# Pacing the sums of weight quarters and splitting the transposes of k and q in a fused retention and MLP kernel

## The chip, the cores and the metric

The kernel runs on one core of one Trainium2 chip. The metric is the device time in microseconds (us), lower is better; a time given for a kernel is the median of its runs. The engines are TensorE (PE, its weight loads PEld), VectorE (DVE), ScalarE (ACT), GpSimd (POOL) and SyncE (SP, which issues the transfers).

## The reference

A retention block (8 batches, 8 heads, 576 positions, head dimension 64) feeds an MLP with a parametric relu, all in float32:

```python
def _attn_ref(q, k, v):                       # q, k, v: (8, 8, 576, 64)
    scores = scale * np.matmul(q, k.transpose(0, 1, 3, 2))
    gamma = 1.0 - 2.0 ** (-5.0 - np.arange(H, dtype=np.float32))
    rel = pos[:, None] - pos[None, :]
    Dmat = np.where(rel >= 0, gamma[:, None, None] ** rel[None, :, :], 0.0)
    return np.matmul(scores * Dmat[None], v)

x = np.ascontiguousarray(attn_out.transpose(0, 2, 1, 3)).reshape(B * S, H * D)   # (4608, 512)
h = x @ w_in                                  # (4608, 2048)
g = np.maximum(h, 0.0) + alpha * np.minimum(h, 0.0)
out = g @ w_out                               # (4608, 512)
```

## The kernel before

The tokens go through the MLP in 18 blocks of 256. Blocks 0 and 1 are multiplied plainly (`plain_unit`, `plain_out`), while the weights are still being loaded and rounded piece by piece (`piece_in` on ScalarE, `piece_out` on VectorE and GpSimd). Every later block uses seven products in the place of eight (`mlp_unit`, the scheme of Strassen and Winograd), and for that the weights need sums and differences of their quarters, which GpSimd makes in place. A block is eight units; a unit is 28 matmuls into `ph` (each float32 product counts as two in the profile), the work on `g`, and 14 matmuls into `po`. The retention goes by pairs of heads, numbered over all batches: pairs 0 to 3 belong to the first batch, 4 to 7 to the second, and so on. Pairs 4 to 7 are computed in the gaps of a loop of 12 plain units, in a fixed order of instructions; pairs 8 to 31 run in a later loop between units of the seven-product kind.

In the excerpts a comment such as `# L304` marks the line under which the profile counts an instruction.

The loads and the sums of the weight quarters. Each quarter of the weights (two units) brings 12 sums, four on `w_in` and eight on `w_out`:

```python
    NEARLY = 2 * NPAIR            # NPAIR = 4
    # ... (cut; load_sq loads in squares of 32 x 32, rows of 32 floats; load_nat in rows of 64)
    def load_pair(n):
        b, c = pairs[n]
        kn, vn, qx = [nat.tile([P, NM, 2, D], FP32, tag=f"nat_{x}", name=f"{x}n_{n}")
                      for x in "kvq"]
        if n < NEARLY:
            kx = kn
            load_nat(kn, k, b, c)
            load_nat(qx, q, b, c)
        else:
            kx = nat.tile([P, NB, 32], FP32, tag="sq_k", name=f"kx_{n}")
            qx = qx.rearrange("p m h d -> p (m h d)")[:, 0:S].rearrange(
                "p (n r) -> p n r", r=32)
            load_sq(kx, k, b, c)
            load_sq(qx, q, b, c)
            load_nat(kn, k, b, c)
        load_nat(vn, v, b, c)
        return kn, kx, qx, vn
    # ... (cut)
    waiting = []
    def combine(n):
        for _ in range(min(n, len(waiting))):
            w, (o, x, y, op) = waiting.pop(0)
            nc.gpsimd.tensor_tensor(out=w[:, o], in0=w[:, x], in1=w[:, y], op=op)  # L304
    S_WORK = ((1, 0, 1, ALU.subtract), (5, 3, 1, ALU.subtract), (4, 5, 0, ALU.add),
              (6, 2, 5, ALU.subtract))
    T_WORK = ((1, 3, 1, ALU.subtract), (5, 1, 0, ALU.add), (4, 3, 5, ALU.subtract),
              (6, 2, 5, ALU.subtract))
    # ... (cut; at the end of plain_out(kb, i, g), after its matmuls into po (L372):)
        if kb == PLAIN[-1] and i % UST == UST - 1:
            waiting.extend((w_in[i // UST], x) for x in S_WORK)
            waiting.extend((w_out[j], x) for j in range(i + 1 - UST, i + 1) for x in T_WORK)
            if i == NU - 1:
                combine(len(waiting))
```

A unit of the seven-product kind (its weights are `w_in[i // 2]` and `w_out[i]`), and the differences of a block's input, which GpSimd makes:

```python
    def combine_x(kb):            # four GpSimd subtractions 128x256 (L425)
        # ... (cut)
    def mlp_unit(kb, i):
        if kb not in xt:
            combine_x(kb)
        x, t = xb[kb], xt[kb]
        ph = [ps_h.tile([P, 4, P], FP32, tag=f"psh{m}", name=f"ph{m}_{kb}_{i}")
              for m in range(2)]
        for n, (m, o, l, r) in enumerate((
                (0, 2, 0, x[:, 0:2, 0:P]), (0, 0, 2, x[:, 2:4, 0:P]), (0, 1, 5, t[:, 1]),
                (1, 0, 4, t[:, 0]), (1, 1, 1, x[:, 0:2, P:TB]),
                (1, 2, 6, x[:, 2:4, P:TB]), (1, 3, 3, t[:, 2]))):
            for cc in range(2):
                nc.tensor.matmul(ph[m][:, o], w_in[i // UST][:, l, i % UST, cc], r[:, cc],  # L439
                                 start=(n in (0, 3) and cc == 0), stop=(n in (2, 6) and cc == 1),
                                 skip_group_check=True)
        g = mlp.tile([P, 8, P], FP32, tag="g", name=f"g_{kb}_{i}")
        nc.scalar.copy(g[:, 7], ph[0][:, 2])  # L445
        for o, x0, x1 in ((g[:, 0:5:4], ph[0][:, 0:2], g[:, 7:8].to_broadcast([P, 2, P])),
                          (g[:, 5:7], ph[1][:, 0:2], g[:, 4:5].to_broadcast([P, 2, P])),
                          (g[:, 3], ph[1][:, 0], g[:, 6]),
                          (g[:, 1:3], ph[1][:, 2:4], g[:, 5:7])):
            nc.vector.tensor_tensor(out=o, in0=x0, in1=x1, op=ALU.add)  # L450
        for m in range(2):
            fc = m * NU + i
            nc.vector.tensor_scalar(g[:, 4 + 2 * m:6 + 2 * m], g[:, 2 * m:2 * m + 2], 0.0,  # L453
                                    alpha[:, fc:fc + 1], ALU.min, ALU.mult)
        nc.vector.scalar_tensor_tensor(  # L455
            out=g[:, 0:4].rearrange("p x t -> p (x t)"),
            in0=g[:, 0:4].rearrange("p x t -> p (x t)"), scalar=0.0,
            in1=g[:, 4:8].rearrange("p x t -> p (x t)"), op0=ALU.max, op1=ALU.add)
        for o, x0, x1, op in ((4, 1, 3, ALU.add), (6, 0, 1, ALU.subtract),
                              (5, 4, 0, ALU.subtract), (7, 2, 5, ALU.subtract)):
            nc.vector.tensor_tensor(out=g[:, o, :], in0=g[:, x0, :], in1=g[:, x1, :], op=op)  # L461
        pend.append((kb, i, g))
        if len(pend) > 1:
            mlp_out()
```

The retention of a pair in its steps, scale, transposes (t), scores (s), states (u) and values (v). The PSUM tiles of all of them share two buffers (`psa`):

```python
    def scale(t, x, c):            # t times its decay factors, two GpSimd multiplications (L510)
        # ... (cut)
    def ps_tile(shape, name):
        return ps_a.tile(shape, FP32, tag="psa", name=name)
    def scale_pair(n):
        c = pairs[n][1]
        scale(loaded[n][2], 0, c)
        scale(loaded[n][3], 1, c)
    def transposes(n):
        c = pairs[n][1]
        kn, kx, qx, vn = loaded[n]
        kT = attn.tile([P, S], FP32, tag="kT", name=f"kT_{n}")
        qT = attn.tile([P, S], FP32, tag="qT", bufs=2, name=f"qT_{n}")
        if n < NEARLY:
            for src, dst in ((kn, kT), (qx, qT)):
                for x, (m0, m1) in enumerate(((0, 3), (3, NM))):
                    w = min(m1 * P, S) - m0 * P
                    pt = ps_tile([P, 3 * P], f"pt{m0}_{n}")
                    for m in range(m0, m1):
                        rows = min(P, S - m * P)
                        nc.tensor.transpose(  # L535
                            pt[:, (m - m0) * P:(m - m0) * P + rows],
                            src[0:rows, m].rearrange("p h d -> p (h d)"),
                            ident[0:rows, 0:rows])
                    nc.scalar.copy(dst[:, m0 * P:m0 * P + w], pt[:, 0:w])  # L539
        else:
            qh = qx.rearrange("p (j x) r -> p j x r", x=2)
            nc.gpsimd.tensor_tensor(out=qh, in0=qh,  # L542
                                    in1=tabx[:, None, c, :, None].to_broadcast([P, NJ, 2, 32]),
                                    op=ALU.mult)
            scale(vn, 1, c)
            for src, dst in ((kx, kT), (qx, qT)):
                nc.vector.transpose(dst, src.rearrange("p n r -> p (n r)"))  # L547
        return kT, qT
    # ... (cut)
    def scores(n, kT, qT):        # two PSUM tiles "psa", 40 matmuls (L565), then
        # ... (cut)               # two DVE operations on them (L569)
    def states(n, kn, vn):
        c = pairs[n][1]
        ps = [ps_tile([P, NM - 1, D], f"pu{p2}_{n}") for p2 in range(2)]
        for m in range(NM - 1):
            for p2 in range(2):
                for h2 in range(2):
                    nc.tensor.matmul(ps[p2][half(h2), m], kn[half(p2), m, h2],  # L580
                                     vn[half(p2), m, h2], start=(m == 0), stop=(m == NM - 2),
                                     skip_group_check=True)
        su = attn.tile([P, NJ - 1, D], FP32, tag="su", bufs=2, name=f"su_{n}")
        g1, g2 = gch[:, 0, c:c + 1], gch[:, 1, c:c + 1]
        nc.scalar.copy(su[:, 0::2], ps[0])  # L585
        nc.vector.scalar_tensor_tensor(out=su[:, 1::2], in0=su[:, 0::2], scalar=g1, in1=ps[1],  # L586
                                       op0=ALU.mult, op1=ALU.add)
        for j in range(3, NJ - 1, 2):
            nc.vector.scalar_tensor_tensor(out=su[:, j], in0=su[:, j - 2], scalar=g2,  # L589
                                           in1=su[:, j], op0=ALU.mult, op1=ALU.add)
        nc.vector.scalar_tensor_tensor(out=su[:, 2::2], in0=su[:, 1:NJ - 3:2], scalar=g1,  # L591
                                       in1=ps[0][:, 1:], op0=ALU.mult, op1=ALU.add)
        return su
    # ... (cut; values: two PSUM tiles "psa", matmuls L604 and L611, then ScalarE copies into xb)
```

The loop of 12 plain units, and the one after it:

```python
    # ... (cut; step("v", n) calls values and then loads pair n + 2)
    steps = [(x, n) for n in range(NPAIR, NEARLY) for x in "tsuv"]
    scale_pair(NPAIR)
    scaled = [NPAIR + 1]
    def gap():
        for x, n in steps[0:3]:
            if x == "t" and n == scaled[0] and n in loaded:
                scaled[0] += 1
                step("scale", n)
        if steps:
            step(*steps.pop(0))
            if not steps:
                combine_x(len(PLAIN))
    units = [(kb, i) for i in range(UST, NU) for kb in PLAIN]
    for n, (kb, i) in enumerate(units):
        plain_unit(kb, i)
        plain_relu()
        if n >= 1:
            gap()
        piece_in(1)
        piece_out(1)
        mlp_out()
        combine(1)
        piece_in(1)
        if n >= 4 or n == 2:
            gap()
        piece_out(1)
        combine(1)
    assert not steps
    ordered.close()
    tc.no_sync_barrier()
    enqueue(0)
    enqueue(1)
    turned = {}
    for n, (b, c) in enumerate(pairs):
        if n < NEARLY:
            continue
        if n + 1 < len(pairs):
            loaded[n + 1] = load_pair(n + 1)
        kn, _, _, vn = loaded[n]
        share = -(-len(queue) // (NPAIR - c))
        cuts = [(share + i) // 3 for i in range(3)][::-1]
        kT, qT = turned.pop(n) if n in turned else transposes(n)
        at = scores(n, kT, qT)
        pop_units(cuts[0])
        su = states(n, kn, vn)
        pop_units(cuts[1])
        if n + 1 < len(pairs):
            turned[n + 1] = transposes(n + 1)
        values(n, vn, qT, at, su)
        del loaded[n]
        pop_units(cuts[2])
```

Of the kernel before, what the change touches and what calls it, by code (L numbers as in the profile page):

```python
# [10 lines left out]
FP32 = mybir.dt.float32  # L11
# [3 lines left out]
ALU = mybir.AluOpType  # L15
# [3 lines left out]
def kernel(  # L19
# [10 lines left out]
    nc = tc.nc  # L30
    B, H, S, D = q.shape
    NTOK, DM = out.shape
    DFF = moe_w_in.shape[1]
    P = 128

    NPAIR = H // 2
    C = 64
    NJ = S // C
    NM = (NJ + 1) // 2
# [3 lines left out]
    NU = NFC // 2  # L43
# [4 lines left out]
    UST = NU // NST  # L48
# [19 lines left out]

    NEARLY = 2 * NPAIR

# [87 lines left out]
    ident = const.tile([P, P], FP32, name="ident")  # L162
# [135 lines left out]

    waiting = []

    def combine(n):
        for _ in range(min(n, len(waiting))):
            w, (o, x, y, op) = waiting.pop(0)
            nc.gpsimd.tensor_tensor(out=w[:, o], in0=w[:, x], in1=w[:, y], op=op)  # L304

    S_WORK = ((1, 0, 1, ALU.subtract), (5, 3, 1, ALU.subtract), (4, 5, 0, ALU.add),
              (6, 2, 5, ALU.subtract))
# [58 lines left out]
    def plain_out(kb, i, g):  # L366
        if i == 0:
            acc[kb] = [ps_o.tile([P, DM], FP32, tag=f"pso{2 * kb + m}", name=f"po{m}_{kb}")
                       for m in range(2)]
        for m in range(2):  # L370
            for x in range(2):
                nc.tensor.matmul(acc[kb][m], g[:, 2 * x + m],  # L372
                                 w_out[i][:, 2 * x:2 * x + 2].rearrange("p x f -> p (x f)"),
                                 start=(i == 0 and x == 0), stop=(i == NU - 1 and x == 1))
        if i == NU - 1:
            po = acc.pop(kb)
            osb = ring.tile([P, 2, DM], FP32, tag=f"o{kb}", name=f"osb_{kb}")
            for m in range(2):
                t0 = kb * TB + m * P
                nc.scalar.copy(osb[:, m], po[m])  # L380
                nc.sync.dma_start(out[t0:t0 + P, :], osb[:, m])
        if kb == PLAIN[-1] and i % UST == UST - 1:
            waiting.extend((w_in[i // UST], x) for x in S_WORK)
            waiting.extend((w_out[j], x) for j in range(i + 1 - UST, i + 1) for x in T_WORK)
            if i == NU - 1:
                combine(len(waiting))

    def plain_unit(kb, i):

# [37 lines left out]
# [31 lines that stand above are left out]
            in1=g[:, 4:8].rearrange("p x t -> p (x t)"), op0=ALU.max, op1=ALU.add)  # L458
        for o, x0, x1, op in ((4, 1, 3, ALU.add), (6, 0, 1, ALU.subtract),
                              (5, 4, 0, ALU.subtract), (7, 2, 5, ALU.subtract)):  # L460
            nc.vector.tensor_tensor(out=g[:, o, :], in0=g[:, x0, :], in1=g[:, x1, :], op=op)  # L461
        pend.append((kb, i, g))
        if len(pend) > 1:
            mlp_out()
# [50 lines left out]
    def ps_tile(shape, name):  # L515
        return ps_a.tile(shape, FP32, tag="psa", name=name)
# [6 lines left out]
    def transposes(n):  # L523
        c = pairs[n][1]
        kn, kx, qx, vn = loaded[n]
        kT = attn.tile([P, S], FP32, tag="kT", name=f"kT_{n}")
        qT = attn.tile([P, S], FP32, tag="qT", bufs=2, name=f"qT_{n}")
        if n < NEARLY:
            for src, dst in ((kn, kT), (qx, qT)):
                for x, (m0, m1) in enumerate(((0, 3), (3, NM))):  # L530
                    w = min(m1 * P, S) - m0 * P
                    pt = ps_tile([P, 3 * P], f"pt{m0}_{n}")
                    for m in range(m0, m1):
                        rows = min(P, S - m * P)
                        nc.tensor.transpose(  # L535
                            pt[:, (m - m0) * P:(m - m0) * P + rows],
                            src[0:rows, m].rearrange("p h d -> p (h d)"),
                            ident[0:rows, 0:rows])
                    nc.scalar.copy(dst[:, m0 * P:m0 * P + w], pt[:, 0:w])  # L539
        else:  # L540
            qh = qx.rearrange("p (j x) r -> p j x r", x=2)
            nc.gpsimd.tensor_tensor(out=qh, in0=qh,  # L542
                                    in1=tabx[:, None, c, :, None].to_broadcast([P, NJ, 2, 32]),
                                    op=ALU.mult)
            scale(vn, 1, c)
            for src, dst in ((kx, kT), (qx, qT)):
                nc.vector.transpose(dst, src.rearrange("p n r -> p (n r)"))  # L547
        return kT, qT

    def half(x):  # L550
        return slice(x * C, (x + 1) * C)
# [252 lines left out]
    plain_unit(0, 1)  # L804
    piece_out(1)
    plain_relu()
    part_values(1)
    part_carry(1)
    piece_in(1)
    last_transposes()  # L810
    mlp_out()
    piece_out(1)
# [20 lines left out]
    def step(what, n):  # L833
        kn, _, _, vn = loaded[n]
        if what == "scale":
            scale_pair(n)
        elif what == "t":
            kq[n] = transposes(n)
        elif what == "s":
            ats[n] = scores(n, *kq[n])  # L840
        elif what == "u":
            sus[n] = states(n, kn, vn)
        elif what == "v":
            values(n, vn, kq[n][1], ats[n], sus[n])
            del loaded[n]
            if n + 2 <= NEARLY:
                loaded[n + 2] = load_pair(n + 2)

    steps = [(x, n) for n in range(NPAIR, NEARLY) for x in "tsuv"]
    scale_pair(NPAIR)  # L850
    scaled = [NPAIR + 1]

    def gap():

        for x, n in steps[0:3]:
            if x == "t" and n == scaled[0] and n in loaded:
                scaled[0] += 1
                step("scale", n)
        if steps:
# [3 lines that stand above are left out]
# [3 lines left out]
# [7 lines that stand above are left out]
        mlp_out()  # L873
        combine(1)
        piece_in(1)
        if n >= 4 or n == 2:
            gap()
        piece_out(1)
        combine(1)
    assert not steps  # L880
    ordered.close()
    tc.no_sync_barrier()
# [2 lines left out]

    turned = {}
    for n, (b, c) in enumerate(pairs):
        if n < NEARLY:
            continue
        if n + 1 < len(pairs):  # L890
            loaded[n + 1] = load_pair(n + 1)
# [13 lines that stand above are left out]
        if c == NPAIR - 1:  # L905
            enqueue(b)
# [31 lines left out]
```

## Time and profile before

| what | value |
|---|---|
| time, median of 3 runs | 1065.72 us (1065.14 to 1067.84) |
| span of the profiled execution | 1063.5 us |
| PE busy | 1026.0 us |
| DVE busy | 765.0 us |
| POOL busy | 215.2 us |
| ACT busy | 171.1 us |
| moved by DMA | 63.36 MB |

A row of the table of groups reads: line, engine, operation, the tile written and those read, shape, count, then busy time, mean time of one, and the idle time of the engine just before. In a timeline, a row begins with its start and its length in us, and ends, in brackets, with the idle time ahead of it and what ended it; several instructions alike are merged. In the chain of waits each step is what released the step after it.

### The profile page before, as it was taken

The numbers are of one execution on the slowest core, as the hardware profiler recorded it, in microseconds if no ns is written. First come the engines' busy times: TensorE is split into PE (matmuls) and PEld (weight loads), VectorE is DVE, ScalarE is ACT, GpSimd is POOL, SyncE is SP. The second block draws the span as 40 slices with busy tenths as digits, with TensorE's granted clock in tenths as the row PEclk, the third lists the DMA queues.
The fourth block names the chain that finished last, engine by engine and source line by source line (L and its number), as shares of the span: only waits on it lengthen the run. The fifth ranks groups of instructions, "written<-read, shape, count | busy, mean of one in ns | idle before, by whom it ended". The sixth has DMA issues, their size and how long they took to land.

```text
span 1063.5 us, 27061 instructions
## 1 busy us (share of the span) xinstructions
PE 1026.0 (96%) x11329; PEld 903.3 (85%) x11329; DVE 765.0 (72%) x1951; ACT 171.1 (16%) x533; POOL 215.2 (20%) x253
## 2 busy tenths in 40 slices
PE   6899997699999999999999999999999999999998
PEld 5666565699999999999999999999999999999997
DVE  7757656877787778676777777777768676767575
ACT  4445541111011111001101111111111111000000
POOL 4455659301120102111103011201120000100000
PEclk9999999799999999999999999999999999999999
DMA  9855504113222222111212222131222100000000
GB/s 244 242 143 155 147 21 107 33 38 77 47 64 46 66 45 56 34 43 35 55 24 55 47 46 66 38 73 36 66 47 55 24 22 1 21 1 22 1 21 20
DMA packets 216073, 63.36 MB, mean 60 GB/s; under 512 B 201088, under 2 KB 209296, under 8 KB 215952
## 3 DMA queue, kind: packets, MB, share of 16 engines
q1 hardware_dynamic: 213840, 61.11, 24.7%
q8 instruction: 89, 1.46, 0.6%
q10 hardware_dynamic: 2112, 0.53, 0.3%
q14 instruction: 32, 0.26, 0.1%
HBM read 52.17 MB, written 9.44 MB: 58 GB/s over the span
## 4 chain that ended last, share of the span: by engine, by line
PE 92%; DVE 4%; issue 1%; POOL 1%; DMA 1%; ACT 0%; SPq 0%; DVEq 0%; POOLq 0%; ACTq 0%
PE ph L439 39%; PE po L357 36%; PE po L372 4%; PE ph L395 4%; PE pv L611 2%; PE ps L565 2%; PE pv L604 2%; DVE g L453 2%; PE pu L580 2%; DMA w_out<-in_k_dram 1%; DVE su L589 1%; DMA kn<-in_k_dram 0%; POOL w_in L294 0%; POOL w_out L294 0%; PE pt L535 0%
## 5 line engine op out<-in xcount | busy, mean ns | idle before, releaser
L357 PE MATMUL po<-w_out,g 128*128 128x256 f32 x1792 | 409.6, 380 | 14.8 <-DVE g L455 14.8
L357 PEld LDWEIGHTS po<-w_out,g 128*128 128x128 f32 x1792 | 332.0, 191 | 55.1 <-DVE g L455 15.0
L450 DVE TENSOR_TENSOR g<-ph,g 128x256 f32<-128x256 f32 (+1 forms) x512 | 187.4, 387 | 179.9 <-PE ph L439 94.9
L439 PE MATMUL ph<-xb,w_in 128*128 128x128 f32 x2048 | 277.6, 278 | 0.0
L439 PEld LDWEIGHTS ph<-xb,w_in 128*128 128x128 f32 x2048 | 253.2, 192 | 9.2 <-issue 1.0
L439 PE MATMUL ph<-xt,w_in 128*128 128x128 f32 x1536 | 213.6, 275 | 0.0
L439 PEld LDWEIGHTS ph<-xt,w_in 128*128 128x128 f32 x1536 | 192.2, 192 | 0.1
L461 DVE TENSOR_TENSOR g<-g 128x128 f32<-128x128 f32 x512 | 142.4, 319 | 7.8
L453 DVE TENSOR_SCALAR g<-g,alpha 128x256 f32<-128x256 f32 x256 | 109.8, 471 | 4.5
L510 POOL TENSOR_TENSOR vn<-vn,th 128x512 f32<-128x512 f32 (+1 forms) x56 | 39.8, 731 | 355.1 <-DMA vn<-in_v_dram 279.1
L445 ACT COPY g<-ph 128x128 f32<-128x128 f32 x128 | 34.1, 266 | 461.7 <-PE ph L439 448.6
L455 DVE SCALAR_TENSOR_TENSOR g<-g 128x512 f32<-128x512 f32 x128 | 91.7, 717 | 3.8
L395 PE MATMUL ph<-xb,w_in 128*128 128x256 f32 x256 | 60.3, 390 | 1.9 <-ACT xb L725 1.4
L372 PE MATMUL po<-w_out,g 128*128 128x512 f32 x128 | 58.8, 602 | 0.8 <-DVE g L411 0.8
L395 PEld LDWEIGHTS ph<-xb,w_in 128*128 128x128 f32 x256 | 48.9, 194 | 11.4 <-issue 4.3
L425 POOL TENSOR_TENSOR xt<-xb,xt 128x256 f32<-128x256 f32 x32 | 25.2, 789 | 162.8 <-ACT xb L500 162.2
L498 ACT COPY xb<-pv 64x64 f32<-64x64 f32 (+1 forms) x144 | 34.0, 236 | 145.7 <-PE pv L611 143.9
L372 PEld LDWEIGHTS po<-w_out,g 128*128 128x128 f32 x128 | 23.3, 190 | 25.0 <-issue 21.8
L411 DVE SCALAR_TENSOR_TENSOR g<-g,nalpha,ph 128x256 f32<-128x256 f32 x32 | 13.9, 477 | 32.1 <-ACT ph L401 32.1
L425 POOL TENSOR_TENSOR xt<-xb 128x256 f32<-128x256 f32 x16 | 11.6, 725 | 117.7 <-PE ph L439 117.7
L547 DVE STREAM_TRANSPOSE qT<-qn 128x576 f32<-128x576 f32 x24 | 18.6, 776 | 23.2 <-PE pv L611 23.2
L542 POOL TENSOR_TENSOR qn<-qn,tabx 128x576 f32<-128x576 f32 x24 | 28.7, 1198 | 31.0 <-DMA qn<-in_q_dram 19.9
(124 smaller groups left out, 665.1 us busy)
## 6 DMA issues: line engine op xcount, KB each, us to landing
out_dram<-osb SPq DMA_DIRECT2D x36, 256.0 KB, 2.2
kn<-in_k_dram SPq DMA_DIRECT2D x56, 128.0 KB, 2.7
vn<-in_v_dram SPq DMA_DIRECT2D x56, 128.0 KB, 2.9
kx<-in_k_dram SPq DMA_DIRECT2D x96, 72.0 KB, 2.4
qn<-in_q_dram SPq DMA_DIRECT2D x96, 72.0 KB, 2.5
raw<-in_moe_w_in_dram SPq DMA_DIRECT2D x24, 256.0 KB, 4.3
raw<-in_moe_w_out_dram SPq DMA_DIRECT2D x10, 512.0 KB, 4.7
w_in<-in_moe_w_out_dram SPq DMA_DIRECT2D x6, 512.0 KB, 4.8
```

Source lines behind the costliest of these rows:

```text
L357: nc.tensor.matmul(acc[kb][n // 2][:, n % 2, :], g[:, x, :], w_out[i][:, y, :], start=(i == 0 and n % 2 == 0), stop=(i == NU - 1 and (n % ...
L372: nc.tensor.matmul(acc[kb][m], g[:, 2 * x + m], w_out[i][:, 2 * x:2 * x + 2].rearrange("p x f -> p (x f)"), start=(i == 0 and x == 0), sto ...
L395: nc.tensor.matmul(ph[:, x], w_in[i // UST][:, cc // 2 * 2 + x, i % UST, cc % 2], xb[kb][:, cc], start=(cc == 0 and x == 0), stop=(cc == N ...
L425: nc.gpsimd.tensor_tensor(out=o, in0=x0, in1=x1, op=ALU.subtract)
L439: nc.tensor.matmul(ph[m][:, o], w_in[i // UST][:, l, i % UST, cc], r[:, cc], start=(n in (0, 3) and cc == 0), stop=(n in (2, 6) and cc == ...
L445: nc.scalar.copy(g[:, 7], ph[0][:, 2])
L450: nc.vector.tensor_tensor(out=o, in0=x0, in1=x1, op=ALU.add)
L453: nc.vector.tensor_scalar(g[:, 4 + 2 * m:6 + 2 * m], g[:, 2 * m:2 * m + 2], 0.0, alpha[:, fc:fc + 1], ALU.min, ALU.mult)
L455: nc.vector.scalar_tensor_tensor(out=g[:, 0:4].rearrange("p x t -> p (x t)"), in0=g[:, 0:4].rearrange("p x t -> p (x t)"), scalar=0.0, in1 ...
L461: nc.vector.tensor_tensor(out=g[:, o, :], in0=g[:, x0, :], in1=g[:, x1, :], op=op)
L498: nc.scalar.copy(to[half(h2)], pv[half(1 - h2), m:m + n])
L510: nc.gpsimd.tensor_tensor(out=t[0:rows, m], in0=t[0:rows, m], in1=th[0:rows, x, None, 2 * c:2 * c + 2, None].to_broadcast([rows, n, 2, D]) ...
```

## The change

The change has five parts. The first spreads the sums of weight quarters: the loop makes three of them per plain unit instead of two, and what is left when the loop ends is no longer made at once; each unit of block 2 (the first of the seven-product kind) makes three after its last VectorE operation, on which they are made to wait. The second makes the transposes of k and of q separate steps, each in a gap of its own. The third loads pairs 6 and 7 (the last two of batch 2) in squares, and VectorE turns them, as it does for pairs 8 to 31; pairs 4 and 5 are still turned by TensorE. The fourth puts the states ahead of the scores, and gives a gap to one more place of the loop, so that 18 steps fit where there were 16. The fifth moves one call that takes a weight piece in ahead of the values of the first batch's second part. It is for keeping GpSimd's long row of sums out of VectorE's way at the start of block 2, and for taking waits and transposes from TensorE.

```diff
--- before.py
+++ after.py
@@ -68,7 +68,7 @@
-    NEARLY = 2 * NPAIR
+    NEARLY = NPAIR + 2
@@ -298,10 +298,14 @@
     waiting = []
-    def combine(n):
+    def combine(n, after=None):
         for _ in range(min(n, len(waiting))):
             w, (o, x, y, op) = waiting.pop(0)
-            nc.gpsimd.tensor_tensor(out=w[:, o], in0=w[:, x], in1=w[:, y], op=op)
+            ins = nc.gpsimd.tensor_tensor(out=w[:, o], in0=w[:, x], in1=w[:, y], op=op)
+            if after is not None:
+                tc.add_manual_dep(ins.ins, after.ins.name, mybir.DependencyInfo(
+                    mybir.DependencyClass.Sync, mybir.DependencyReason.DATA),
+                    reason="sums of the last stage follow the units of a block")
     S_WORK = ((1, 0, 1, ALU.subtract), (5, 3, 1, ALU.subtract), (4, 5, 0, ALU.add),
               (6, 2, 5, ALU.subtract))
@@ -382,8 +386,6 @@
         if kb == PLAIN[-1] and i % UST == UST - 1:
             waiting.extend((w_in[i // UST], x) for x in S_WORK)
             waiting.extend((w_out[j], x) for j in range(i + 1 - UST, i + 1) for x in T_WORK)
-            if i == NU - 1:
-                combine(len(waiting))
     def plain_unit(kb, i):
@@ -458,7 +460,10 @@
             in1=g[:, 4:8].rearrange("p x t -> p (x t)"), op0=ALU.max, op1=ALU.add)
         for o, x0, x1, op in ((4, 1, 3, ALU.add), (6, 0, 1, ALU.subtract),
                               (5, 4, 0, ALU.subtract), (7, 2, 5, ALU.subtract)):
-            nc.vector.tensor_tensor(out=g[:, o, :], in0=g[:, x0, :], in1=g[:, x1, :], op=op)
+            ins = nc.vector.tensor_tensor(out=g[:, o, :], in0=g[:, x0, :], in1=g[:, x1, :], op=op)
+
+        combine(3, ins)
+        assert i < NU - UST or not waiting
         pend.append((kb, i, g))
         if len(pend) > 1:
             mlp_out()
@@ -525,27 +530,30 @@
         kn, kx, qx, vn = loaded[n]
         kT = attn.tile([P, S], FP32, tag="kT", name=f"kT_{n}")
         qT = attn.tile([P, S], FP32, tag="qT", bufs=2, name=f"qT_{n}")
-        if n < NEARLY:
-            for src, dst in ((kn, kT), (qx, qT)):
-                for x, (m0, m1) in enumerate(((0, 3), (3, NM))):
-                    w = min(m1 * P, S) - m0 * P
-                    pt = ps_tile([P, 3 * P], f"pt{m0}_{n}")
-                    for m in range(m0, m1):
-                        rows = min(P, S - m * P)
-                        nc.tensor.transpose(
-                            pt[:, (m - m0) * P:(m - m0) * P + rows],
-                            src[0:rows, m].rearrange("p h d -> p (h d)"),
-                            ident[0:rows, 0:rows])
-                    nc.scalar.copy(dst[:, m0 * P:m0 * P + w], pt[:, 0:w])
-        else:
-            qh = qx.rearrange("p (j x) r -> p j x r", x=2)
-            nc.gpsimd.tensor_tensor(out=qh, in0=qh,
-                                    in1=tabx[:, None, c, :, None].to_broadcast([P, NJ, 2, 32]),
-                                    op=ALU.mult)
-            scale(vn, 1, c)
-            for src, dst in ((kx, kT), (qx, qT)):
-                nc.vector.transpose(dst, src.rearrange("p n r -> p (n r)"))
+        qh = qx.rearrange("p (j x) r -> p j x r", x=2)
+        nc.gpsimd.tensor_tensor(out=qh, in0=qh,
+                                in1=tabx[:, None, c, :, None].to_broadcast([P, NJ, 2, 32]),
+                                op=ALU.mult)
+        scale(vn, 1, c)
+        for src, dst in ((kx, kT), (qx, qT)):
+            nc.vector.transpose(dst, src.rearrange("p n r -> p (n r)"))
         return kT, qT
+
+    def turn(n, i):
+
+        src = loaded[n][i]
+        dst = attn.tile([P, S], FP32, tag="qT" if i else "kT", bufs=2 if i else 1,
+                        name=f"T{i}_{n}")
+        for m0, m1 in ((0, 3), (3, NM)):
+            w = min(m1 * P, S) - m0 * P
+            pt = ps_tile([P, 3 * P], f"pt{i + m0}_{n}")
+            for m in range(m0, m1):
+                rows = min(P, S - m * P)
+                nc.tensor.transpose(pt[:, (m - m0) * P:(m - m0) * P + rows],
+                                    src[0:rows, m].rearrange("p h d -> p (h d)"),
+                                    ident[0:rows, 0:rows])
+            nc.scalar.copy(dst[:, m0 * P:m0 * P + w], pt[:, 0:w])
+        return dst
     def half(x):
         return slice(x * C, (x + 1) * C)
@@ -804,9 +812,9 @@
     plain_unit(0, 1)
     piece_out(1)
     plain_relu()
+    piece_in(1)
     part_values(1)
     part_carry(1)
-    piece_in(1)
     last_transposes()
     mlp_out()
     piece_out(1)
@@ -836,6 +844,8 @@
             scale_pair(n)
         elif what == "t":
             kq[n] = transposes(n)
+        elif what in "kq":
+            kq[n] = kq.get(n, ()) + (turn(n, 0 if what == "k" else 2),)
         elif what == "s":
             ats[n] = scores(n, *kq[n])
         elif what == "u":
@@ -843,17 +853,18 @@
         elif what == "v":
             values(n, vn, kq[n][1], ats[n], sus[n])
             del loaded[n]
-            if n + 2 <= NEARLY:
+            if n + 2 <= 2 * NPAIR:
                 loaded[n + 2] = load_pair(n + 2)
-    steps = [(x, n) for n in range(NPAIR, NEARLY) for x in "tsuv"]
+    steps = [(x, n) for n in range(NPAIR, 2 * NPAIR)
+             for x in ("kqusv" if n < NEARLY else "tusv")]
     scale_pair(NPAIR)
     scaled = [NPAIR + 1]
     def gap():
         for x, n in steps[0:3]:
-            if x == "t" and n == scaled[0] and n in loaded:
+            if x == "k" and n == scaled[0] and n in loaded:
                 scaled[0] += 1
                 step("scale", n)
         if steps:
@@ -873,10 +884,10 @@
         mlp_out()
         combine(1)
         piece_in(1)
-        if n >= 4 or n == 2:
+        if n >= 2:
             gap()
         piece_out(1)
-        combine(1)
+        combine(2)
     assert not steps
     ordered.close()
     tc.no_sync_barrier()
@@ -885,7 +896,7 @@
     turned = {}
     for n, (b, c) in enumerate(pairs):
-        if n < NEARLY:
+        if n < 2 * NPAIR:
             continue
         if n + 1 < len(pairs):
             loaded[n + 1] = load_pair(n + 1)
```

## Prediction

> **What bounds the kernel now.** I read the page's engine rows and slices first, then the table of stretches of 20 us over the first 200, then the chain of waits, and last the timelines of single engines where a stretch had a hole. The page:
>
> ```profile
> PE 1026.0 (96%) x11329; PEld 903.3 (85%) x11329; DVE 765.0 (72%) x1951; ACT 171.1 (16%) x533; POOL 215.2 (20%) x253
> ...
> PE   6899997699999999999999999999999999999998
> ...
> PEclk9999999799999999999999999999999999999999
> ```
>
> TensorE is the bound, and only 37.5 of 1063.5 us are left in which it does nothing. So I ask where those lie. Each digit covers 26.6 us: the first slice and the seventh and eighth (160 to 213 us) are the weak ones. The table of stretches (the columns are the stretch, its length, and busy time with the count of PE, PEld, DVE, ACT and POOL, then TensorE's granted clock, DMA share and GB/s) puts figures on them:
>
> ```profile
> 100.00:120.00 20.00, 18.62 (x231) 12.41 (x230) 13.52 (x23) 9.67 (x25) 10.68 (x12) 1.00 0.47 145
> 120.00:140.00 20.00, 18.23 (x225) 11.98 (x225) 13.52 (x22) 9.59 (x26) 12.25 (x12) 1.00 0.64 145
> 140.00:160.00 20.00, 19.85 (x230) 12.90 (x231) 10.48 (x22) 8.70 (x24) 9.42 (x12) 1.00 0.01 2
> 160.00:180.00 20.00, 19.36 (x133) 13.79 (x131) 11.20 (x13) 3.97 (x8) 19.84 (x24) 1.00 0.39 86
> 180.00:200.00 20.00, 5.87 (x49) 4.71 (x50) 19.37 (x19) 0.27 (x1) 12.94 (x17) 0.66 0.27 57
> ```
>
> From 180 to 200 TensorE works 5.87 us of 20 and its clock falls to 0.66. From 60 to 169, the loop of plain units, it works 103.72 of 109, a loss of 5.3 us. From 200 to 1063 it works 859.25 of 863, so the long rest offers nothing; the first 40 us lose 11.4, but the change hardly touches them. The hole at 180 to 200 in the timelines of VectorE, GpSimd (parts) and TensorE (a row is start, length, then the instructions):
>
> ```profile
> 173.30 0.62 DVE L450 TENSOR_TENSOR g<-ph,g 128x128 f32<-128x128 f32 x2
> 173.96 19.39 DVE L453 TENSOR_SCALAR g<-g,alpha 128x256 f32<-128x256 f32 x2
> 193.38 0.69 DVE L455 SCALAR_TENSOR_TENSOR g<-g 128x512 f32<-128x512 f32 x1
> ```
>
> ```profile
> 178.71 2.48 POOL L304 TENSOR_TENSOR w_in<-w_in 128x512 f32<-128x512 f32 x2
> 181.16 0.72 POOL L304 TENSOR_TENSOR w_out<-w_out 128x256 f32<-128x256 f32 x1
> ...
> 191.80 1.14 POOL L542 TENSOR_TENSOR qn<-qn,tabx 128x576 f32<-128x576 f32 x1
> ```
>
> ```profile
> 178.75 0.61 PE L439 MATMUL ph<-xt,w_in 128*128 128x128 f32 x4
> 194.13 1.22 PE L357 MATMUL po<-w_out,g 128*128 128x256 f32 x2 [14.77 <-DVE g L455]
> ```
>
> Two VectorE instructions, whose median over the kernel is 352 ns each, take 19.39 us. They end at 193.35, when GpSimd's unbroken row ends (191.80 + 1.14 = 192.94). TensorE waits 14.77 us for their unit. The row is the sums that the loop didn't make. From 159.7 on, line L304 has 21 sums on w_out (median 0.719 us) and 8 on w_in (1.262), the loop's last five on w_out among them; the other 24 are 16 x 0.719 + 8 x 1.262 = 21.6 us, with input differences and scalings of the next pairs between them.
>
> The 5.3 us of the loop are two waits, here from TensorE's timeline:
>
> ```profile
> 117.29 0.80 PE L535 MATMUL pt<-ident,kn 128*128 128x128 f32 x5
> 119.08 0.83 PE L535 MATMUL pt<-ident,qn 128*128 128x128 f32 x5 [0.99 <-POOL w_out L304]
> ```
>
> ```profile
> 112.32 0.69 PE L604 MATMUL pv<-at,vn 64*64 64x64 f32 x32 [0.39 <-DVE su L591]
> ```
>
> The first comes for each of the four pairs, 4 x 0.99 = 3.96 us. The profile names GpSimd, with a different line each time; the code says that q's transposes need one of the two shared PSUM buffers back, which ScalarE's copy of k (118.50 to 119.20) frees. I take the copy. The second comes for two pairs, 0.39 and 0.93 us: values needs the buffer that L591, last of the states chain, still reads.
>
> **What the Trainium skill says.** "SBUF — State Buffer", section "SBUF: two separate sides": VectorE and GpSimd share a port pair under an exclusive lock, held for a whole instruction, while the other blocks. "VectorE: DVE Perf Modes", section "Mode 2×_2P — use both read ports for one tensor": a float32 tensor-scalar on SBUF can take both read ports. Together they name L453, whose operands are SBUF tiles, as the one that can be shut out, and L450, which reads PSUM, as one that isn't. The trace agrees: two L450 ran in 0.62 us at 173.30 under the same row of sums. It adds that a lock of single instructions can starve the other engine for 19 us when the row has no break. "TensorE: Matmul & The Clock Gate", section "What's actually happening": after an idle window of about 3.4 us the clock halves. The trace has 0.66 as mean clock in that stretch, and the first 14 matmuls after the hole take 4.94 us, against 3.02 for the next 14 in the chain.
>
> **The change, part by part.**
>
> 1. Pacing. In 12 plain units the old loop has places for 2 x 12 = 24 sums, the new one for 36. There are 4 quarters x 12 = 48, of which the last 12 are released only after the loop. So 24 were left at the end before, 12 now, and those fall three at a time behind units 1 to 4 of block 2. The first three are on w_in, 3 x 1.26 = 3.8 us, then 2.7 and twice 2.2. A unit's last VectorE instruction and the next unit's L453 are apart by 4.4 us (199.75 to 204.17 in the timeline), so each group fits or almost does. With 3.3 us for the next unit's ph and 3.0 for the po before it, a unit lasts 6.3 us on TensorE, against 3.9 on VectorE (4 L450 1.57, L453 0.61, L455 0.69, L461 1.02); the slack of 2.4 us takes what sticks out. Removed: **14.8** us of waiting and 4.94 - 3.02 = **1.9** of cold clock. Left over, as an allowance for groups that join with a scaling: **-0.8**.
> 2. More sums in the loop: GpSimd there is busy 65.3 of 109 us; twelve sums on w_in and w_out are 4 x 1.26 + 8 x 0.72 = 10.8 more, so about 76. TensorE doesn't wait for them, since no plain unit reads a sum. **0**.
> 3. Squares for pairs 6 and 7. Off TensorE: 2 pairs x (0.80 + 0.83) = **3.3** us, all on the path. Onto VectorE: 2 x 2 transposes of 0.77 = 3.1 us, into a loop where it is busy 64.7 of 109. ScalarE loses 2 x 1.4 us. The pair loads another copy of k: 4 issues, some 2 to 3.4 us of SyncE. Pair 7 is loaded after the values of pair 5 and needed five gaps later, some 20 us. **3.3**.
> 4. k and q apart: between the two lies a po of 3.6 us, in which the copies of k (0.70) end. For pairs 4 and 5 the wait goes by this, for 6 and 7 by part 3: **4.0**.
> 5. States before scores: the same two buffers are now wanted by scores one gap after states, so I expect the wait of 1.3 us to move, not to go, and to grow a little where GpSimd's longer rows delay L589 (three took 0.93 us at 151.46 and 2.52 at 130.39). **0**, give or take 1.5.
> 6. The moved weight piece lies in the first 45 us, where ScalarE idles 2.94 us ahead of the copy at 42.29: **0**.
>
> Sum: 14.8 + 1.9 - 0.8 + 3.3 + 4.0 = 23.2 us. 1065.7 - 23.2 = **1042.5 us**.
>
> **Rivals.** *The lock moves into block 2.* Groups of sums, the differences of block 3 (four of 0.72) and the scalings of pairs 9 and 10 (1.14 + 1.39) could still form one row without a break and hold L453 for more than the slack. For it: in the old row these were interleaved just so, from 181 to 193. Against it: the sums wait for the unit, so that a row of 2.2 + 2.9 + 2.5 = 7.6 us is about the longest, 7.6 - 4.4 - 2.4 = 0.8 past the slack. Even two or three of these make 1045. *The loop becomes bound by something else.* With 8 us less on TensorE it could wait for weight pieces, for loads in short rows, or for GpSimd's scaling of v ahead of states, which for pairs 6 and 7 is now one gap before its use, behind up to 4 us of other GpSimd work. The pieces are two units ahead and DMA is used at half, which speaks against it; the scaling of v is the weak place. It makes 1045 to 1048. *All of the waits go,* the states' too, and nothing takes their place: 1065.7 - 14.8 - 1.9 - 3.3 - 5.3 = 1040.4, and with a better start 1038.
>
> **Range and chances.** The 16.7 us of the hole are the sure part, the 3.3 of the transposes nearly so. The least I can see is these with half of the rest eaten, 1048; the most is 1038. The range is 1038 to 1047.5. The mark of 2% is 1044.4, which the expected value passes by 1.9 us only. Chances: 0.68 faster by over 2%, 0.31 within, 0.01 slower.
>
> **What would show it.** Right: no TensorE idle of over 1 us between 155 and 190; L453's longest under 4 us, not 19; the sums in threes in block 2; TensorE busy about 1021 us (1026.0 - 3.3 - 1.9); 20 L535 matmuls instead of 40; no wait of 0.99 ahead of q's transposes; small waits ahead of scores (L565) in place of values (L604). Wrong: L453 over 6 us in block 2, TensorE waiting for L455 there; or idle time ahead of states (L580) on GpSimd's L510, or ahead of plain units (L395) on a weight piece.

## The result and the profile after

The changed kernel takes 1049.39 us (median of 4 runs, 1047.74 to 1051.22) against 1065.7 before (4 runs): a ratio of 0.9844, 95% interval 0.982 to 0.9868. It is 16.3 us faster, where 23.2 were predicted, and lies above the predicted range of 1038 to 1047.5.

The change shifts the line numbers. In the changed kernel a unit's tensor-scalar is L455 (L453 before), the states chain L594, L597, L599 (L586, L589, L591), states' matmuls L588, scores' L573, values' L612, the scaling of q L534 and of v L515, and VectorE's transposes L539.

The page of the changed kernel, engines and slices:

```profile
PE 1021.1 (98%) x11309; PEld 899.7 (86%) x11309; DVE 753.4 (72%) x1955; ACT 168.6 (16%) x525; POOL 215.5 (21%) x251
...
PE   5899989999999999999999999999999999999998
```

The hole at the seventh and eighth digit has become full, and TensorE's busy time is the 1021 us that the prediction gave. The table of stretches says where TensorE still idles (after the length: busy time of PE, PEld, DVE, ACT, POOL, then TensorE's clock):

```profile
120.00:140.00 20.00, 17.45 (x221) 11.51 (x220) 14.11 (x25) 9.08 (x22) 11.68 (x13) 1.00 0.67 132
140.00:160.00 20.00, 15.72 (x214) 10.39 (x213) 11.63 (x20) 5.62 (x16) 14.96 (x16) 1.00 0.01 2
160.00:180.00 20.00, 20.00 (x139) 14.89 (x139) 9.63 (x24) 3.96 (x8) 9.91 (x14) 1.00 0.46 110
180.00:200.00 20.00, 20.00 (x290) 17.99 (x289) 15.91 (x38) 3.07 (x13) 12.03 (x13) 1.00 0.52 94
```

From 160 to 200 nothing is lost; L455's longest instruction is 1.593 us, not 19. From 120 to 160, 6.83 us are lost, more than the 5.3 of the whole loop before. TensorE's timeline of the changed kernel has four waits there, and no other from 60 to 200:

```profile
124.08 0.79 PE L588 MATMUL pu<-vn,kn 64*64 64x64 f32 x32 [2.07 <-POOL vn L515]
129.24 0.80 PE L573 MATMUL ps<-qT,kT 64*64 64x64 f32 x38 [0.48 <-DVE su L599]
144.90 0.79 PE L588 MATMUL pu<-vn,kn 64*64 64x64 f32 x32 [2.60 <-POOL vn L515]
151.26 0.81 PE L573 MATMUL ps<-qT,kT 64*64 64x64 f32 x38 [1.68 <-DVE su L599]
```

They belong to pairs 6 and 7, which the change has VectorE turn. The first needs the scaled v. GpSimd's timeline of the changed kernel:

```profile
119.95 1.29 POOL L294 TENSOR_TENSOR w_in<-w_in,raw 128x512 int32<-128x512 int32 x1 [3.53 <-DMA kx<-in_k_dram]
121.21 0.72 POOL L304 TENSOR_TENSOR w_out<-w_out 128x256 f32<-128x256 f32 x1
121.89 1.14 POOL L534 TENSOR_TENSOR qn<-qn,tabx 128x576 f32<-128x576 f32 x1
122.99 1.39 POOL L515 TENSOR_TENSOR vn<-vn,th 128x512 f32<-128x512 f32 x2
```

v stands behind a weight piece, a sum and the scaling of q, all of which start only at 119.95. VectorE's timeline of the same moments:

```profile
119.13 0.69 DVE L292 SCALAR_TENSOR_TENSOR w_in<-raw,wc 128x512 int32<-128x512 int32 x1
119.74 0.77 DVE L539 STREAM_TRANSPOSE kT<-kx 128x576 f32<-128x576 f32 x1
123.06 0.78 DVE L539 STREAM_TRANSPOSE qT<-qn 128x576 f32<-128x576 f32 x1 [2.55 <-POOL qn L534]
123.77 0.67 DVE L287 TENSOR_SCALAR wc<-wa 128x512 f32<-128x512 f32 x1
...
126.59 0.47 DVE L594 SCALAR_TENSOR_TENSOR su<-su,gch,pu 128x256 f32<-128x256 f32 x1
127.10 1.67 DVE L597 SCALAR_TENSOR_TENSOR su<-su,gch 128x64 f32<-128x64 f32 x3
128.69 0.40 DVE L599 SCALAR_TENSOR_TENSOR su<-su,gch,pu 128x192 f32<-128x192 f32 x1
```

VectorE stands still for 2.55 us until GpSimd has scaled q, and a weight piece, the relu and the states chain queue up behind that transpose. So two waits stand side by side: TensorE's for v, and VectorE's for q. GpSimd's row starts as late as 119.95 because its first instruction, the weight piece, goes on with what VectorE's L292 writes, and that ends at 119.82 (119.13 + 0.69). The DMA named on GpSimd's line loads k, which the piece doesn't read.

### The profile page after: what moved, and what is told of

It reads as the page before. It is cut to its first block, busy times and chain, and to the rows that moved or that the text cites. A ratio compares the mean times of both kernels' runs of the same rounds, so it can differ in the third digit from the quotient of the medians.

```text
span 1046.0 us, 27044 instructions
## 1 busy us (share of the span) xinstructions
PE 1021.1 (98%) x11309; PEld 899.7 (86%) x11309; DVE 753.4 (72%) x1955; ACT 168.6 (16%) x525; POOL 215.5 (21%) x251
## 4 chain that ended last, share of the span: by engine, by line
PE 86%; DVE 1%; issue 1%; ACT 0%; POOL 0%; DVEq 0%; POOLq 0%
PE ph L441 40%; PE po L361 37%; PE pv L619 2%; PE ps L573 2%; PE pv L612 2%; PE pu L588 1%; PE ph L397 1%; PE po L376 1%; DVE su L597 0%; POOL qn L534 0%; DVE g L413 0%; DVE wc L290 0%; DVE wc L287 0%; POOL w_in L304 0%; ACT wa L276 0%
## 5 line engine op out<-in xcount | busy, mean ns | idle before, releaser
L515 POOL TENSOR_TENSOR vn<-vn,th 128x512 f32<-128x512 f32 (+1 forms) x56 | 39.7, 730 | 337.5 <-DMA vn<-in_v_dram 313.1
L455 DVE TENSOR_SCALAR g<-g,alpha 128x256 f32<-128x256 f32 x256 | 92.6, 403 | 4.5
L376 PEld LDWEIGHTS po<-w_out,g 128*128 128x128 f32 x128 | 23.2, 190 | 25.0 <-issue 22.2
L539 DVE STREAM_TRANSPOSE qT<-qn 128x576 f32<-128x576 f32 x26 | 20.2, 777 | 29.2 <-PE pv L619 23.2
L534 POOL TENSOR_TENSOR qn<-qn,tabx 128x576 f32<-128x576 f32 x26 | 31.7, 1218 | 26.7 <-DMA qn<-in_q_dram 15.0
```

Source lines behind the costliest of these rows:

```text
L376: nc.tensor.matmul(acc[kb][m], g[:, 2 * x + m], w_out[i][:, 2 * x:2 * x + 2].rearrange("p x f -> p (x f)"), start=(i == 0 and x == 0), sto ...
L515: nc.gpsimd.tensor_tensor(out=t[0:rows, m], in0=t[0:rows, m], in1=th[0:rows, x, None, 2 * c:2 * c + 2, None].to_broadcast([rows, n, 2, D]) ...
```

## The experiments

Three theories. A: the loss comes from where pairs 6 and 7 have their scaling, in the step of the transposes, one gap ahead of states. B: it comes from the third sum per unit, which fills GpSimd. C: the loads in squares land late (GpSimd's line above names a DMA). All times are medians, with the interval of the ratio to the kernel before; the changed kernel stands at 1049.39. The runs number their lines differently: with the scaling ahead the scores are L581 and the states chain L602, L605 and L607; with v alone ahead they are L576 and L597, L600 and L602; with the sums alone the chain is L591, L594 and L596.

### Scaling given out ahead

```diff
 def gap():
     for x, n in steps[0:3]:
-        if x == "k" and n == scaled[0] and n in loaded:
+        if x == ("k" if n < NEARLY else "t") and n == scaled[0] and n in loaded:
             scaled[0] += 1
-            step("scale", n)
+            if n < NEARLY: step("scale", n)
+            else: scale_sq(n); ahead.add(n)   # v and q of a pair in squares
 def transposes(n):
-    (scaling of q, scaling of v)
+    if n not in ahead: scale_sq(n)
```

> The changed kernel, with the scaling of v and q of pairs 6 and 7 given out up to three steps ahead of the transposes (as for pairs 4 and 5) instead of in the step of the transposes. Theory A (the scaling of v comes one gap ahead of states, last in GpSimd's order): the two waits ahead of states, 2.07 + 2.60 us, vanish, those ahead of scores (0.48 + 1.68) may stay; 1049.4 - 4.7 = 1044.7 us. Rival B (GpSimd is too full with a third sum per unit, wherever the scaling stands): the waits stay or move, within 1 us of 1049.4. Rival C (the loads in squares land too late): GpSimd waits for a DMA ahead of the scaling, 1049 or more.

Measured: 1042.37 us, ratio 0.9792 (0.977 to 0.9815), 7.0 us below the changed kernel. TensorE's timeline of this run, from 60 to 200 us, has one wait left:

```profile
145.65 0.81 PE L581 MATMUL ps<-qT,kT 64*64 64x64 f32 x38 [1.26 <-DVE su L607]
```

A holds, with more than it expected, since 0.90 of the 2.16 us of waits ahead of scores went too. In the profiled runs the gain is 5.6 us (spans of 1046.0 and 1040.4), just these 4.67 + 0.90. B and C are out as the cause of the waits ahead of states: sums and loads are unchanged, and the scaling for pair 6 now starts at 113.38 and ends at 115.88 without a DMA to wait for.

### v alone, and the order of v and q

Which of the two scalings matters? One run gives out v's alone ahead, the other swaps the two in their step.

```diff
 # v alone ahead: the hook as above, but only scale(vn, 1, c); in transposes:
-    scale(vn, 1, c)
+    if n not in ahead: scale(vn, 1, c)
 # v before q, in transposes:
-    scale q; scale(vn, 1, c)
+    scale(vn, 1, c); scale q
```

> The changed kernel with the scaling of v alone (1.39 us) given out up to three steps ahead; that of q stays in the step of the transposes. If v's lateness is the cause by itself, both waits ahead of states go and nothing comes in their place: 1049.4 - 4.7 = 1044.7 us. If q's lateness is the deeper one (GpSimd's scaling of q, VectorE's transpose behind it, and behind that in VectorE's order the relu and the chain of states), the waits ahead of states go but those ahead of scores grow by about as much, to some 2.5 and 3.5 us: 1048 to 1050 us.

Measured: 1051.6 us, ratio 0.9868 (0.9852 to 0.9884), no gain on the changed kernel: by the medians it is 2.2 us slower, but the intervals overlap. Its TensorE timeline:

```profile
127.66 0.32 PE L576 MATMUL ps<-qT,kT 64*64 64x64 f32 x2 [0.85 <-DVE su L597]
129.77 1.34 PE L576 MATMUL ps<-qT,kT 64*64 64x64 f32 x38 [1.78 <-DVE su L602]
149.91 0.32 PE L576 MATMUL ps<-qT,kT 64*64 64x64 f32 x2 [1.39 <-DVE su L597]
153.22 1.24 PE L576 MATMUL ps<-qT,kT 64*64 64x64 f32 x38 [2.98 <-DVE su L602]
```

The waits ahead of states went, and 7.0 us of waits ahead of scores stand where there were 6.83 us of both kinds. The time is above the 1048 to 1050 expected; in this trace VectorE still waits 2.56 us for q, and the clock of TensorE fell to one half for 3.4 us around each pair of waits, on which more at the end.

> The changed kernel with one order reversed: in the transposes of a pair GpSimd scales v (1.39 us) ahead of q (1.14 us). Theory A in its simple form (only the place of v in GpSimd's row counts): the waits ahead of states shrink by 1.14 us each, 1049.4 - 2.3 = 1047.1 us. A in the form that VectorE's order carries it on: VectorE's transpose of q now ends 1.4 us later, and the chain of states stands behind it, so that the waits ahead of scores grow by 1 to 2.5 us each and eat the gain: 1048.5 to 1050.

Measured: 1054.39 us, ratio 0.9886 (0.9872 to 0.9901), slower than both forms of the theory expected. The waits ahead of states fell to 0.97 and 1.50, those ahead of scores rose to 1.06 + 1.77 and 1.07 + 2.98: 9.35 in all. Both runs say that my theory A named the lesser half. It is the scaling of q that holds up VectorE, whose order then carries the delay to the states chain, and that chain frees the buffer for which scores wait. Bringing v forward lets TensorE reach that wait sooner, no more. Between v alone ahead and both ahead little but the place of q's scaling differs, and the waits fall from 7.0 us to 1.26. (q alone ahead was not run.)

### States ahead of the transposes

```diff
-             for x in ("kqusv" if n < NEARLY else "tusv")]
+             for x in ("kqusv" if n < NEARLY else "utsv")]   # with the scaling ahead
```

> As the run with the scaling ahead, and pairs 6 and 7 in the order states, transposes, scores, values: the transposes need no PSUM buffer, so that scores come two gaps after states. Theory A: all four waits vanish, 2.07 + 2.60 + 0.48 + 1.68 = 6.8 us, 1042.6 us. If the wait ahead of scores is not for the buffer that the chain of states still reads, but for the transposed q, it stays: 1044 or more. Rival B: 1049.

Measured: 1041.8 us, ratio 0.9775 (0.9759 to 0.9791). The wait for the buffer is gone, but 0.80 and 1.28 us ahead of scores are now for VectorE's transpose of q, which stands behind the states chain. It is no clear gain on 1042.37.

### The four pairs on TensorE

```diff
-    NEARLY = NPAIR + 2
+    NEARLY = 2 * NPAIR
```

> The changed kernel without its third part: all four pairs of batch 2 turned by TensorE, k and q apart. Theory A: no wait ahead of states, 20 more transposes (3.3 us) on TensorE; 1049.4 - 4.7 + 3.3 = 1048.0 us, or 1046 if the waits ahead of scores go too. Rival B: the waits stay and the transposes come on top, 1052.7 us.

Measured: 1046.83 us, ratio 0.9826 (0.9812 to 0.9841). The loop has no wait at all, although it makes three sums per unit: the third sum by itself, B, doesn't make the loop's four waits. One wait stands at the start of block 2, where pair 8 meets the same chain through q:

```profile
168.08 0.81 PE L573 MATMUL ps<-qT,kT 64*64 64x64 f32 x40 [2.31 <-DVE qT L539]
```

So the squares, as the change has them, cost 2.6 us by the medians (1049.39 - 1046.83; the intervals overlap) in place of the 3.3 that they should bring, and that against a run with this wait of its own.

### The sums alone, and all but the sums

```diff
 # alone: the kernel before with combine(n, after), combine(3, ins) in mlp_unit,
 # combine(2) in the loop, and without the last
-            if i == NU - 1: combine(len(waiting))
```

> The kernel before with the first part of the change alone (three sums per unit in the loop, the last twelve behind units of block 2). Theory A: the hole of 14.8 us and the 1.9 us of cold clock go, the loop stays as it was: 1065.7 - 16.7 = 1049.0 us. Rival B: the third sum makes the loop wait by 4 us or more, 1053 us. If the lock only moves into block 2: 1055 or more, with L453 over 6 us there.

Measured: 1050.93 us, ratio 0.986 (0.9846 to 0.9875). The hole is gone and block 2 has no wait, but the waits ahead of values grew from 1.32 us to 1.87 + 1.07 + 0.20 = 3.14. For the longest, VectorE's and GpSimd's timelines of this run:

```profile
109.04 3.46 DVE L594 SCALAR_TENSOR_TENSOR su<-su,gch 128x64 f32<-128x64 f32 x3
```

```profile
107.42 2.64 POOL L304 TENSOR_TENSOR w_in<-w_in 128x512 f32<-128x512 f32 x2
110.03 1.39 POOL L515 TENSOR_TENSOR qn<-qn,th 128x512 f32<-128x512 f32 x2
```

A row of two sums, with the scaling of q and v right behind it, holds up the chain. B has this much right: the third sum costs 1.8 us of waits in the old order of steps (3.14 - 1.32).

> The changed kernel with the first part undone: two sums per unit in the loop, the rest at once when the loop ends. If the pacing carries the gain of the hole, L455 (the tensor-scalar of a unit) is shut out for some 19 us again, TensorE waits about 14 us in block 2, and the time is 1049.4 + 16.7 = 1066 us, less up to 1.5 us where fewer sums meet the chain of states in the loop: 1064.5 to 1066. If the other parts had removed the hole: 1049.

(The edit undoes the first part in the changed kernel.) Measured: 1065.53 us over 12 runs, ratio 0.9996 (0.9985 to 1.0007), so the other four parts by themselves bring nothing. TensorE's timeline has the hole back, and the clock's share with it (6.17 us for 14 matmuls):

```profile
195.02 6.17 PE L361 MATMUL po<-w_out,g 128*128 128x256 f32 x14 [15.75 <-DVE g L459]
```

In the loop, with two sums per unit again, the waits ahead of states stay (2.61 and 2.06) and those ahead of scores are gone.

### How many sums, and when

> The changed kernel with two sums per unit in the loop, as before the change, and the other 24 behind units of block 2, five to a unit. Rival B (the third sum fills GpSimd): all four waits of the loop go, 1042.6 us. Theory A: the waits ahead of states stay (4.0 to 4.7 us), those ahead of scores shrink to under 1 us together; rows of 5 sums are at most 5.8 us, inside 4.4 + 2.4 us of room, so no new wait in block 2: 1047.5 to 1049 us.

(`combine(1)` for `combine(2)` in the loop, `combine(5, ins)` in the units.) Measured: 1047.95 us, ratio 0.9824 (0.9808 to 0.9841). The waits ahead of states stay, 2.61 and 2.07, and those ahead of scores vanish: the third sum has a part in these, as the run with the sums at once shows too. Five sums in a row put a wait of 0.76 us ahead of values in block 2, again through q: VectorE waits 3.11 us there for GpSimd's L534, which stands behind them. The time is within the noise of the changed kernel's.

In the next run the two counts of sums in a loop unit are swapped, with the scaling ahead. VectorE's and GpSimd's timelines of the run with the scaling ahead show what it aims at:

```profile
142.33 2.85 DVE L605 SCALAR_TENSOR_TENSOR su<-su,gch 128x64 f32<-128x64 f32 x3
```

```profile
142.49 2.61 POOL L304 TENSOR_TENSOR w_in<-w_in 128x512 f32<-128x512 f32 x2
```

> The run with the scaling ahead (1042.4 us), and the counts of sums in a unit of the loop swapped: two after the first weight piece, one after the second. In that run the last wait, 1.26 us ahead of scores of pair 7, came with two sums on w_in (142.49 to 145.10) that held up three L605 of the states chain for 2.85 us. If the lock is that cause, the chain takes about 1.0 to 1.6 us and the wait goes: 1041 us. If not, 1042.4.

Measured: 1041.34 us, ratio 0.9767 (0.9753 to 0.9782). The three L605 took 2.27 us, not 1.0 to 1.6, with a weight piece and one sum of GpSimd still beside them; the wait fell from 1.26 to 0.68, not to nothing.

> The run with the scaling ahead (1042.4 us), with two sums per unit in the loop and the other 24 behind units of block 2, four to a unit. The theory says that the last wait of that run (1.26 us) is two sums on w_in meeting the chain of states; with two a unit, one at a time, it goes: 1041 us. The cost would be in block 2, where rows of up to 5 us may hold up a chain of states or a tensor-scalar, as the run with five behind showed 0.76 us: then 1041.5 to 1042.5, no better than with the counts swapped (1041.3).

Measured: 1040.88 us, ratio 0.9766 (0.975 to 0.9782), the lowest of the medians, though not distinct from the one before. One wait of 0.24 us is left in the loop, and from 165 to 200 us TensorE is never idle.

### The wait ahead of the second transposes, and the fifth part

The four waits of 0.99 us in the kernel before stand ahead of q's transposes. Here q is turned first:

```diff
-            for src, dst in ((kn, kT), (qx, qT)):      # the kernel before
+            for src, dst in ((qx, qT), (kn, kT)):
```

> The kernel before with k and q turned in the other order, q first. If the 0.99 us ahead of the second set of transposes is for a PSUM buffer that ScalarE's copy of the first set frees, the same 0.99 us now stands ahead of k's transposes, four times, and the time stays at 1065.5. If it is GpSimd (which scales q and not k, and which the profile names), k's transposes wait for nothing and the four waits go or stand ahead of q.

Measured, one run: 1065.12 us. TensorE's timeline, the same for all four pairs:

```profile
118.76 0.86 PE L535 MATMUL pt<-ident,kn 128*128 128x128 f32 x5 [0.94 <-ACT qT L539]
```

k isn't scaled by anybody, so the wait is for the buffer that ScalarE's copy frees, and the profile of the kernel before named the wrong engine.

> The run with the counts swapped (1041.3 us) with the fifth part of the change undone: the weight piece taken in after the values of the second part, as before. If the fifth part is worth nothing, TensorE's waits of the first 60 us and the time stay within the noise of one run, 1040.5 to 1043; if it kept ScalarE off the path, a new wait of 0.5 us or more stands between 40 and 50 us.

Measured, one run: 1039.69 us, with TensorE's waits of 0.93 and 0.27 us between 40 and 43 where the run with the counts swapped has 1.47 and 0.27. The fifth part brings nothing that a single run can show.

## Why the prediction was wrong

**Step 1, the hole: right.** 14.8 + 1.9 us were expected; undoing this part alone costs 1065.53 - 1049.39 = 16.1. The allowance of 0.8 was not needed: in the changed kernel the groups of three leave no wait in block 2.

**Step 3, the squares: this step failed.** The prediction put 3.3 us on the path and the work that replaces it beside it, because VectorE and GpSimd had free time. TensorE did lose the 20 transposes. But a pair that VectorE turns needs q scaled before the transpose, while a pair that TensorE turns had q and v scaled far ahead. The scaling was now given out in the step itself, behind a weight piece that starts late, and VectorE waited for it (2.55 and 3.09 us) with the states chain queued behind. With 3.3 expected and -2.6 measured, against the run with all four pairs on TensorE, this step is by the medians 5.9 us off, most of the miss of 6.9. With v and q given out ahead the kernel takes 1042.37 us and keeps one wait of 1.26, close to the 1042.5 and the 1.3 of the prediction: the place of the scaling was missing from it, and nothing large besides.

The second rival had named the scaling of v as the weak place and priced such losses at 1045 to 1048, and idle time ahead of states on GpSimd's scaling of v, the sign that the prediction gave for being wrong, is what came. Step 3 itself weighed free time instead of order. The rival did look at the order, but missed q: moving v alone brought nothing.

**Step 2, the third sum: off by a little.** "TensorE doesn't wait for them" was true of the sums as operands, not of what they hold up. L589 has two SBUF inputs; "SBUF — State Buffer", section "SBUF: two separate sides", of the Trainium skill says that such an operation is shut out too, against a GpSimd operation that reads SBUF. The trace agrees: three took 0.93 us with GpSimd idle and 2.85 under two sums. The cost was 1.8 us with the sums alone; in the changed kernel it shows as the waits ahead of scores (2.16 us), which two sums per unit remove. Scaling ahead lowers them too, so this cost and that of step 3 overlap.

**Step 4, k and q apart: right.** The four waits are gone, also where all four pairs are turned by TensorE, and the run with q first bears out the copy as their cause. **Step 5, states before scores: half right.** It named the place to which the wait would move, but at pair 5 it went altogether (0.39 before); pairs 6 and 7 wait 0.48 and 1.68 us where pair 6 waited 0.93. The growth from 1.32 to 2.16 in all is inside the allowance of 1.5. **Step 6: right,** as far as a single run shows.

The range had a slip of its own. The hole's 16.7 us and the transposes' 3.3, which the prediction called sure and nearly so, make 1045.7 us, so that 1048 as the least gain, and 1047.5 as the end of the range, don't follow from them. The changed kernel lies above either.

In the profiled runs all that lies ahead of block 2 brought 1.0 us (TensorE's first product of block 2 starts at 167.58, not 168.58), and what follows, the hole above all, the other 16.5 of 17.5. Theory A stands with its main term changed from v to q, and what is left of B is that the third sum holds up the chain.

## What to carry to other kernels

An engine with free time is no free engine: what you give it runs in its order, and the question is which instruction ahead in that order starts last, and which behind it somebody needs. If an instruction that waits for another engine is put into an in-order stream, give out what it waits for several steps ahead, here a gain of 7.0 us (5.6 in the profiled runs) for moving the scaling of v and q of two pairs. A long row of work on GpSimd is to be broken up, above all ahead of a tensor-scalar on SBUF: one L453 of the old row took 19.13 us and ended at 193.09, just after the row (192.94). The states chain got one between two sums: in the run with five sums in a row, two L597 that start at 183.90 end at 185.05, while the row goes on from 183.56 to 187.03.

## What had not been expected of the hardware

Short waits can cost TensorE its clock as well, but their length alone doesn't decide. In the run with v before q the 38 matmuls after waits of 1.06 + 1.77 and of 1.07 + 2.98 us took 1.12 and 1.34 us in place of 0.81. In the run with the sums at once the clock fell after a single wait of 2.06 us, while the profiled run of the changed kernel kept it at 1.00 through waits of 2.07 and 2.60. The traces show why: within a run the clock, 1 or one half, changes only in steps of 3.41 us, and what counts is how busy TensorE was in the step before. The first two lines are two such steps of the run with the sums at once, the other two of the changed kernel (TensorE's busy time stands behind the length, the clock is the third figure from the end):

```profile
142.86:146.27 3.41, 1.34 (x8) 0.84 (x6) 1.04 (x2) 1.08 (x2) 3.41 (x5) 1.00 0.01 2
146.27:149.69 3.42, 3.42 (x35) 2.20 (x36) 3.28 (x8) 1.51 (x3) 1.75 (x3) 0.50 0.00 0
```

```profile
143.32:146.73 3.41, 1.83 (x35) 1.29 (x36) 2.78 (x5) 1.14 (x4) 1.88 (x3) 1.00 0.01 2
146.73:150.15 3.42, 2.85 (x9) 0.99 (x7) 3.31 (x6) 0.51 (x1) 3.22 (x3) 1.00 0.00 0
```

Busy for 1.34 of 3.41 us, TensorE lost half its clock in the next step; busy for 1.83, it did not. In all fourteen traces of this case a step at full clock that was busy to 45% or less was followed by one at half (37 steps), and a step of 60% or more never was; in between both occur. So the clock doesn't wait for a step that is idle throughout, as the prediction took it, and one and the same wait can fall into one step or be shared by two. In its four runs the changed kernel's mean clock was 0.996, 0.995, 0.993 and 0.993 at 1047.74, 1048.18, 1050.6 and 1051.22 us. That the slower two lost such a step is likely but not shown, since their traces were not taken.
